# Early loads with one issue per tensor, weight gates from a DMA schedule, and a last tile in two column halves, in a kernel of local attention followed by a two-product MLP

## The chip, the cores and the metric

The kernel runs on one core of one Trainium2 chip. The metric is device time in microseconds (us), as the median of several executions. The "span" of a profile is the time from its first to its last instruction; an execution is about 1.8 us longer than its span.

Engine names in the profile: PE is TensorE's matmuls, PEld its weight loads, DVE is VectorE, ACT is ScalarE, POOL is GpSimd, SP is SyncE. A name with q (SPq, POOLq) is that engine's instruction sequencer, which also issues DMAs.

## The reference

Four batches of 768 positions, eight heads of 64. Each query sees the 96 positions up to itself and the first eight positions of its batch; the result goes through an MLP with `h - tanh(h)` in the middle.

```python
def _attn_ref(q, k, v, n_global, n_local):      # (4, 8, 768, 64), n_global 8, n_local 96
    scores = scale * np.matmul(q, k.transpose(0, 1, 3, 2)) + bias   # bias: -slope(head) * distance
    scores = np.where(keep, scores, -1000000000.0)                  # keep: global or local
    ...                                                             # softmax
    return np.matmul(a, v)

def _moe_ref(x, w_in, w_out):                   # x (3072, 512), w_in (512, 2048), w_out (2048, 512)
    h = x @ w_in
    g = h - np.tanh(h)
    return g @ w_out
```

## The kernel before

The 3072 tokens are 24 tiles of 128. Each tile is loaded as three tensors of 256 KB (keys, queries, values), cast to bf16, transposed on TensorE (early tiles) or by DMA (later tiles), and goes through scores, exponential, product with the values (called AV below), division, transposition, first product with w_in, tanh and difference, and second product with w_out. Each weight matrix comes in four quarters, which GpSimd loads with a cast to bf16 (1 MiB read, 512 KB written, per quarter).

All instructions are ordered by a small planner in the kernel: it simulates the five engines with estimated durations and emits each engine's instructions in the order found. An engine then runs strictly in that order. Three parts matter here. First, the early loads, where keys and queries of the first four tiles are issued as two halves each:

```python
    def load(u, nm, src, dst):
        ...
        if u < PE_B and nm != "vf":          # PE_B = 4
            for a in range(2):
                started(("ld", nm, u), nc.sync.dma_start(
                    out=dst[u][a * Dh : (a + 1) * Dh].rearrange("p t d -> p (t d)"),
                    in_=rows[a * NP : (a + 1) * NP].rearrange("h (k t) d -> k h (t d)", t=H),
                ))
        else:
            started(("ld", nm, u), nc.sync.dma_start(out=dst[u], in_=rows.rearrange("h p d -> p h d")))
```

Second, the order of loads, with "gates": a gated load is issued only when another one has landed. Here the first w_in quarter waits for the fourth tile's keys, and dummy matmuls on a tile of zeros (`warm`) keep TensorE busy before there is work:

```python
    before = [
        ("t", 0), ("t", 1), ("t", 2), ("t", 3), ("in", 0), ("in", 1), ("in", 2), ("in", 3), ("out", 0),
        ("out", 1), ("t", 4), ("out", 2), ("out", 3), ("t", 5), ("t", 6), ("t", 7),
    ]
    ...
    for n, it in enumerate(before):
        if n and it[0] != "t" and before[n - 1][0] == "t":
            gate_of[it] = ("ld", "kf", before[n - 1][1])
        elif n >= 2 and it[0] == "t" and before[n - 1][0] != "t":
            gate_of["ld", "kf", it[1]] = landed(before[n - 2])
```

Third, the end of each tile: sixteen matmuls of 128x512 into one PSUM bank, one copy by ScalarE, one store.

```python
    def m2_e(u):
        ots[u] = opool.tile([P, DM], FP32, name="ot")
        nc.scalar.copy(out=ots[u], in_=os_.pop(u))

    def store(u):
        nc.sync.dma_start(out=out[u * P : (u + 1) * P, :], in_=ots.pop(u))
```

The softmax here doesn't subtract the row's maximum and nothing guards it: scores larger than these inputs give would overflow.

## Time and profile before

| | before |
|---|---|
| median of 3 runs, us | 224.93 (224.05 to 225.29) |
| span of the profiled execution, us | 221.7 |
| first matmul with w_in starts | 21.56 |
| first w_in quarter: issued, landed | 15.8, 21.5 |
| last matmul ends, span ends | 217.86, 221.7 |

From the profile's page, the span and the part "chain that ended last", which is followed back from the last instruction and gives each engine's share:

```profile
span 221.7 us, 5261 instructions
...
PE 85%; DMA 6%; SPq 4%; issue 2%; ACT 1%; POOL 1%; DVE 1%; POOLq 0%
```

TensorE has 85% of the chain. What is not TensorE is at the two ends. The next view is the table of stretches of before; after the stretch and its length come each engine's busy time in us (with its number of instructions), the granted clock of TensorE, the mean busy share of the 16 DMA engines and what they moved:

```profile
core 0: us, PE busy (x) PEld busy (x) DVE busy (x) ACT busy (x) POOL busy (x), PEclk, DMA share, GB/s
...
14.00:16.00 2.00, 1.55 (x17) 0.67 (x16) 1.48 (x4) 1.51 (x2) 1.42 (x3) 1.00 0.78 191
16.00:18.00 2.00, 2.00 (x59) 1.53 (x58) 1.18 (x5) 1.23 (x2) 2.00 (x4) 1.00 0.19 35
18.00:20.00 2.00, 1.95 (x25) 0.98 (x24) 1.28 (x3) 1.41 (x2) 2.00 (x4) 1.00 1.09 172
```

There is a hole: in the stretch from 16 to 18 us the DMA engines are 0.19 busy, although all the weights are still to come. The timeline of GpSimd (start, length, engine, line, operation; in brackets the idle time before it and what ended it) shows why:

```profile
14.39 0.62 POOL L186 CAST vb_107<-vf 128x512 bf16<-128x512 f32 x1 [1.23 <-DMA vf<-in_v_dram]
15.19 0.61 POOL L178 CAST kq<-kf 128x512 bf16<-128x512 f32 x1 [0.19 <-DMA kf<-in_k_dram]
15.75 0.89 POOL L168 DMA_DIRECT2D w_in_bf_97<-in_moe_w_in_dram  x1
```

GpSimd, which must issue the weights, first waits for the third tile's values, casts them, and then waits for the fourth tile's keys. The timeline of TensorE shows the 21 dummies and the late first matmul with w_in:

```profile
1.20 6.22 PE L317 MATMUL one<-zero 128*128 128x512 bf16 x21 [1.20 <-DVE zero L577]
7.34 0.69 PE L198 MATMUL one<-ident,kq 64*64 64x64 bf16 x32
...
21.56 1.08 PE L325 MATMUL one<-xT,w_in_bf_97 128*128 128x128 bf16 x16 [0.82 <-DMA w_in_bf_97<-in_moe_w_in_dram]
```

At the end, the timeline shows the last copy, of 0.58 us, after which the span has another 3.2 us, with the store:

```profile
217.90 0.58 ACT L359 COPY ot<-one 128x512 f32<-128x512 f32 x1 [2.87 <-PE one L352]
```

### The profile page before, as it was taken

What the parts mean: (1) busy time and instruction counts of PE and PEld (TensorE: products, weight loads), DVE (VectorE), ACT (ScalarE), POOL (GpSimd) and SP (SyncE); (2) the same over time, 40 slices, a digit from 0 to 9 for tenths busy, and PEclk for the clock granted to TensorE, in tenths of its full rate; (3) what the DMA queues carried; (4) which work ended last, traced back from release to release, by engine and by line L of the source; (5) the groups of instructions that cost most, each with busy time, mean ns of one, the idle gap of its engine ahead of it and who ended that gap; (6) DMA issues with size and microseconds to landing.
All of it is one profiled execution on the core that took longest, in us unless ns stands there. A gap on an engine that the chain in (4) does not pass through costs nothing.

```text
span 221.7 us, 5261 instructions
## 1 busy us (share of the span) xinstructions
PE 211.8 (96%) x2084; PEld 133.7 (60%) x2113; DVE 135.0 (61%) x278; ACT 127.5 (58%) x212; POOL 52.9 (24%) x85
## 2 busy tenths in 40 slices
PE   7788999999999999999999999999999999999993
PEld 3455897659686566566556555656656555555541
DVE  7246575456788789788886866677566444444300
ACT  5176567837689377575764666656764454534321
POOL 1468003126455453143322323321000000000000
PEclk9999999999999999999999999999999999999999
DMA  4988998999999999999999999993621111001112
GB/s 125 244 202 141 204 216 165 183 213 240 270 230 239 219 231 209 194 206 191 251 173 198 243 214 231 164 234 72 121 71 27 47 47 47 27 27 47 47 65 77
DMA packets 96409, 35.21 MB, mean 159 GB/s; under 512 B 89728, under 2 KB 91776, under 8 KB 96384
## 3 DMA queue, kind: packets, MB, share of 16 engines
q1 hardware_dynamic: 93696, 30.68, 65.5%
q0 software_dynamic: 2688, 4.19, 10.8%
q8 instruction: 16, 0.26, 0.5%
q14 instruction: 9, 0.07, 0.1%
HBM read 27.26 MB, written 6.29 MB: 151 GB/s over the span
## 4 chain that ended last, share of the span: by engine, by line
PE 85%; DMA 6%; SPq 4%; issue 2%; ACT 1%; POOL 1%; DVE 1%; POOLq 0%
PE one L325 38%; PE one L352 37%; PE big L242 5%; DMA w_in_bf_98<-in_moe_w_in_dram 4%; SPq L159 3%; PE big L265 2%; DMA vf<-in_v_dram 2%; PE big L269 2%; PE one L204 1%; PE one L292 1%; SPq L164 1%; POOL kq L178 1%; ACT pd L250 0%; DVE g L342 0%; DVE pd L254 0%
## 5 line engine op out<-in xcount | busy, mean ns | idle before, releaser
L336 ACT ACTIVATE th<-one 128x384 f32<-128x384 f32 (+1 forms) x120 | 61.3, 514 | 52.6 <-PE one L325 51.7
L342 DVE TENSOR_TENSOR g<-one,th 128x384 bf16<-128x384 f32 (+1 forms) x120 | 68.2, 581 | 38.4 <-ACT th L336 37.1
L352 PEld LDWEIGHTS <-g 128*128 128x128 bf16 x384 | 36.2, 98 | 34.3 <-issue 0.2
L180 POOL CAST kq<-kf 128x512 bf16<-128x512 f32 x20 | 13.2, 660 | 72.0 <-DMA kf<-in_k_dram 69.1
L250 ACT ACTIVATE pd<-big 128x1024 bf16<-128x1024 f32 x24 | 24.5, 1025 | 9.9 <-PE big L242 9.8
L325 PE MATMUL one<-xT,w_in_bf_97 128*128 128x128 bf16 (+1 forms) x192 | 25.5, 273 | 0.8 <-DMA w_in_bf_97<-in_moe_w_in_dram 0.8
L325 PE MATMUL one<-xT,w_in_bf_98 128*128 128x128 bf16 (+1 forms) x192 | 25.5, 273 | 0.2 <-DMA w_in_bf_98<-in_moe_w_in_dram 0.2
L325 PE MATMUL one<-xT,w_in_bf_99 128*128 128x128 bf16 (+1 forms) x192 | 25.6, 273 | 0.0
L325 PE MATMUL one<-xT,w_in_bf_100 128*128 128x128 bf16 (+1 forms) x192 | 25.2, 273 | 0.1
L352 PE MATMUL one<-w_out_bf_101,g 128*128 128x512 bf16 x89 | 24.1, 379 | 0.5 <-DVE qk L216 0.2
L359 ACT COPY ot<-one 128x512 f32<-128x512 f32 x24 | 14.1, 588 | 16.9 <-PE one L352 16.7
L352 PE MATMUL one<-w_out_bf_103,g 128*128 128x512 bf16 x90 | 23.5, 379 | 0.3
L352 PE MATMUL one<-w_out_bf_104,g 128*128 128x512 bf16 x89 | 23.3, 379 | 0.5 <-issue 0.2
L352 PE MATMUL one<-w_out_bf_102,g 128*128 128x512 bf16 x90 | 23.4, 379 | 0.3
L254 DVE TENSOR_TENSOR pd<-pd,mk 128x1024 bf16<-128x1024 bf16 x20 | 15.4, 771 | 10.2 <-ACT pd L250 9.9
L250 ACT ACTIVATE po<-big 128x1024 bf16<-128x1024 f32 x20 | 20.5, 1027 | 0.5 <-PE big L242 0.5
L325 PEld LDWEIGHTS <-w_in_bf_97 128*128 128x128 bf16 x192 | 16.1, 114 | 7.0 <-DMA w_in_bf_97<-in_moe_w_in_dram 0.9
L325 PEld LDWEIGHTS <-w_in_bf_100 128*128 128x128 bf16 x192 | 16.3, 113 | 6.4 <-issue 0.2
L325 PEld LDWEIGHTS <-w_in_bf_99 128*128 128x128 bf16 x192 | 16.2, 114 | 6.5
L325 PEld LDWEIGHTS <-w_in_bf_98 128*128 128x128 bf16 x192 | 16.0, 114 | 6.5 <-DMA w_in_bf_98<-in_moe_w_in_dram 0.3
L278 DVE TENSOR_TENSOR x<-big,rden 128x512 bf16<-128x512 f32 x24 | 16.6, 692 | 0.9
L180 POOL CAST kq<-qf 128x512 bf16<-128x512 f32 x20 | 14.2, 711 | 8.2 <-DMA qf<-in_q_dram 8.1
(100 smaller groups left out, 189.3 us busy)
## 6 DMA issues: line engine op xcount, KB each, us to landing
vf<-in_v_dram SPq DMA_DIRECT2D x24, 256.0 KB, 4.5
out_dram<-ot SPq DMA_DIRECT2D x24, 256.0 KB, 2.7
kf<-in_k_dram SPq DMA_DIRECT2D x20, 256.0 KB, 3.6
qf<-in_q_dram SPq DMA_DIRECT2D x20, 256.0 KB, 4.3
kf<-in_k_dram SPq DMA_DIRECT2D x8, 128.0 KB, 3.6
qf<-in_q_dram SPq DMA_DIRECT2D x8, 128.0 KB, 3.4
w_in_bf_97<-in_moe_w_in_dram POOLq DMA_DIRECT2D x1, 512.0 KB, 5.8
w_in_bf_98<-in_moe_w_in_dram POOLq DMA_DIRECT2D x1, 512.0 KB, 8.1
```

Source lines behind the costliest of these rows:

```text
L159: started(("ld", nm, u), nc.sync.dma_start(out=dst[u][a * Dh : (a + 1) * Dh].rearrange("p t d -> p (t d)"), in_=rows[a * NP : (a + 1) * NP ...
L180: eng.tensor_copy(out=kq[u][:, j, :].rearrange("p (c a d) -> p a c d", a=2, d=Dh), in_=t.rearrange("p (a c) d -> p a c d", a=2),)
L242: nc.tensor.matmul(s[:, hh * NP + p, :], qk[u - o][r, 1, p, :], qk[u][r, 0, p, :], start=(u >= PE_B), stop=(u >= PE_B or p == NP - 1),)
L250: nc.scalar.activation(pr[u, o], s, AF.Exp, bias=0.0, scale=scale)
L254: nc.vector.tensor_tensor(out=pr[u, o], in0=pr[u, o], in1=mk[:, :, m, :], op=ALU.mult)
L265: nc.tensor.matmul(dst, pr[u, 0][:, h, :], vb[u % NV][:, h, :], start=True, stop=last,)
L278: nc.vector.tensor_tensor(out=xs[u].rearrange("q (a h) d -> q a h d", a=2), in0=t[:, :, :, 0:Dh], in1=rden.to_broadcast([P, 2, H // 2, Dh] ...
L325: nc.tensor.matmul(t[:, (f - f0) * n : (f - f0 + 1) * n], w_in_bf[j][:, c, i : FJ * P : FJ], xT[b][:, c, o : o + n], start=(c == 0), stop= ...
L336: nc.scalar.activation(h_view(ths[g, f0], g), h_view(hs[g, f0], g), AF.Tanh, bias=0.0, scale=1.0)
L342: nc.vector.tensor_tensor(out=gs[b][:, f0 : f0 + m, o : o + n], in0=h_view(hs.pop((g, f0)), g), in1=h_view(ths.pop((g, f0)), g), op=ALU.su ...
L352: nc.tensor.matmul(os_[u], gs[u // HT][:, f, t * P : (t + 1) * P], w_out_bf[f // FJ][:, f % FJ, :], start=(f == 0), stop=(f == CF - 1),)
L359: nc.scalar.copy(out=ots[u], in_=os_.pop(u))
```

## The change

The intent: give SyncE half as many early issues, so that the DMA engines are kept full; compute the gates from a simple schedule of the DMA engines, so that weights are issued before the last early load has landed; and shorten the end by finishing half of the last tile's columns earlier. With it come settings for the middle (bias by matmul for a fifth tile, transposes by DMA from the tenth tile in place of the eleventh, `AHEAD` 4.5, `EARLY2` 6), and the first w_out quarter moves to second place among the weights. Cut to its core:

```diff
-    PE_B = 4
-    PE_T, PE_X = 10, 10
+    PE_B = 5
+    LB = 4
+    PE_T, PE_X = 9, 9
...
-    EARLY, EARLY2 = 6, 4
+    EARLY, EARLY2 = 6, 6
...
+    BY_ACT = [("qf", 0)]
...
-        if u < PE_B and nm != "vf":
-            for a in range(2):
-                started(("ld", nm, u), nc.sync.dma_start(
-                    out=dst[u][a * Dh : (a + 1) * Dh].rearrange("p t d -> p (t d)"),
-                    in_=rows[a * NP : (a + 1) * NP].rearrange("h (k t) d -> k h (t d)", t=H),
-                ))
+        eng = nc.scalar if (nm, u) in BY_ACT else nc.sync
+        if u < LB and nm != "vf":
+            started(("ld", nm, u), eng.dma_start(
+                out=dst[u].rearrange("p t d -> p (t d)"),
+                in_=rows.rearrange("h (k t) d -> k h (t d)", t=H),
+            ))
...
+    def a_TL(u, j):                     # early transposes, keys and queries apart, as 128x64 matmuls
+        tr[u, j] = ps_one.tile([P, NP * P], FP32, name="one")
+        for t in range(H):
+            for a in range(2):
+                nc.tensor.matmul(
+                    tr[u, j][a * Dh : (a + 1) * Dh, t * Dh : (t + 1) * Dh],
+                    kq[u][:, j, t * Dh : (t + 1) * Dh],
+                    ident.rearrange("p (k a c) -> p a k c", a=2, c=NP)[:, a], start=True, stop=True,
+                )
...
-    AHEAD = 6.0
-    WARM = (1.4, 19.0)
+    AHEAD = 4.5
+    WARM = (1.3, 16.0)
...
-        ("t", 0), ("t", 1), ("t", 2), ("t", 3), ("in", 0), ("in", 1), ("in", 2), ("in", 3), ("out", 0),
+        ("t", 0), ("t", 1), ("t", 2), ("t", 3), ("in", 0), ("out", 0), ("in", 1), ("in", 2), ("in", 3),
...
+    T_LAND, T_SP, T_POOL = 1.0, 1.6, 2.2
+    ends = []
+    at = 2.3
+    for n, it in enumerate(before):
+        first = ("ld", "kf", it[1]) if it[0] == "t" else it
+        if n and (it[0] == "t") != (before[n - 1][0] == "t"):
+            due = at + 0.3 - T_LAND - (T_SP if it[0] == "t" else T_POOL)
+            past = [key for e, key in ends if e <= due]
+            if past:
+                gate_of[first] = past[-1]
+        ...                             # at grows by the estimated transfer; its end goes to `ends`
...
-        e0 = DVE if u == 0 else POOL
-        c0 = 0.5 if u == 0 else 0.62
+        e0, c0 = ((DVE, POOL), (0.48, 0.62)) if u < PE_B else ((POOL,), (0.62,))
...
+        if u == NU - 1:                 # the last tile: two halves of 256 columns
+            for qq in range(4):
+                d, r = divmod(qq, 2)
+                op(("m2", u, qq), PE, 0.88, lambda u=u, d=d, r=r: m2_half(u, d, r), ...)
+            for d, e, us in ((0, ACT, 0.4), (1, DVE, 0.28)):
+                op(("ev", u, d), e, us, lambda u=u, d=d, e=e: m2_half_e(e, u, d), ...)
+                op(("st", u, d), SP, 0.45, lambda u=u, d=d: store_half(u, d), ...)
+            continue
```

With these gates the first w_in quarter waits for the third tile's queries.

More of the change, by code (lines that the diff above doesn't have):

```diff
@@ L154, in load @@
         rows = src[b, :, i * P : (i + 1) * P, :]
-        if u < PE_B and nm != "vf":
-            for a in range(2):
-                started(("ld", nm, u), nc.sync.dma_start(
-                    out=dst[u][a * Dh : (a + 1) * Dh].rearrange("p t d -> p (t d)"),
-                    in_=rows[a * NP : (a + 1) * NP].rearrange("h (k t) d -> k h (t d)", t=H),
-                ))
+        eng = nc.scalar if (nm, u) in BY_ACT else nc.sync
[4 more added lines that the diff above has]
+            ))
         else:
-            started(("ld", nm, u), nc.sync.dma_start(out=dst[u], in_=rows.rearrange("h p d -> p h d")))
+            started(("ld", nm, u), eng.dma_start(out=dst[u], in_=rows.rearrange("h p d -> p h d")))
     def load_w_in(j):
@@ L176, in cast @@
         t = src.pop(u)
-        if u < PE_B:
+        if u < LB:
             eng.tensor_copy(out=kq[u][:, j, :], in_=t.rearrange("p h d -> p (h d)"))
@@ L193, in a_T @@
         for j in (1, 0):
-            if u < PE_B:
-                for t in range(H):
-                    for a in range(2):
-                        r = slice(a * Dh, (a + 1) * Dh)
-                        nc.tensor.transpose(
-                            tr[u][r, j].rearrange("r c f -> r (c f)")[:, t * Dh : (t + 1) * Dh],
-                            kq[u][r, j, t * Dh : (t + 1) * Dh], ident[r, r],
-                        )
-                continue
             for p in range(NP):
                 nc.tensor.transpose(tr[u][:, j, p, :], kq[u][:, j, p * P : (p + 1) * P], ident)
+    def a_TL(u, j):
[7 more added lines that the diff above has]
+                )
     def a_DT(u):
@@ L220, in a_Te @@
             qk[u] = kpool.tile([P, 2, NP, P], BF16, name="qk")
-        if u < PE_B:
+        if u < LB:
             copy(e, out=qk[u][:, j].rearrange("r c (k t) -> r c k t", t=H),
-                 in_=tr[u][:, j].rearrange("r c f -> r (c f)").rearrange(
-                     "r (t k c) -> r c k t", t=H, c=NP))
+                 in_=tr.pop((u, j)).rearrange("r (t k c) -> r c k t", t=H, c=NP))
         else:
@@ L355, in m2, with m2_half, m2_half_e, store_half @@
             )
+    def m2_half(u, d, r):
+        if r == 0:
+            os_[u, d] = ps_one.tile([P, DM], FP32, name="one")
+        t = u % HT
+        w = DM // 2
+        for f in range(r * CF // 2, (r + 1) * CF // 2):
+            nc.tensor.matmul(
+                os_[u, d][:, 0:w], gs[u // HT][:, f, t * P : (t + 1) * P],
+                w_out_bf[f // FJ][:, f % FJ, d * w : (d + 1) * w], start=(f == 0), stop=(f == CF - 1),
+            )
+    def m2_half_e(e, u, d):
+        w = DM // 2
+        ots[u, d] = opool.tile([P, w], FP32, name=f"oh{d}")
+        copy(e, out=ots[u, d], in_=os_.pop((u, d))[:, 0:w])
+    def store_half(u, d):
+        w = DM // 2
+        nc.sync.dma_start(out=out[u * P : (u + 1) * P, d * w : (d + 1) * w], in_=ots.pop((u, d)))
     def m2_e(u):
@@ L369 @@
     before = [
-        ("t", 0), ("t", 1), ("t", 2), ("t", 3), ("in", 0), ("in", 1), ("in", 2), ("in", 3), ("out", 0),
+        ("t", 0), ("t", 1), ("t", 2), ("t", 3), ("in", 0), ("out", 0), ("in", 1), ("in", 2), ("in", 3),
         ("out", 1), ("t", 4), ("out", 2), ("out", 3), ("t", 5), ("t", 6), ("t", 7),
     ]
-    def landed(it):
-        return ("ld", "vf", it[1]) if it[0] == "t" else it
     tiles = [it[1] for it in before if it[0] == "t"]
+    T_LAND, T_SP, T_POOL = 1.0, 1.6, 2.2
[8 more added lines that the diff above has]
+                gate_of[first] = past[-1]
+        if it[0] == "t":
+            for nm in ("kf", "qf", "vf"):
+                at += T_LD if it[1] >= LB or nm == "vf" else T_LD8
+                ends.append((at, ("ld", nm, it[1])))
+        else:
+            at += T_W[it[0]]
+            ends.append((at, it))
     for u in range(NU):
@@ L381 @@
             tiles.append(u)
-    for n, it in enumerate(before):
-        if n and it[0] != "t" and before[n - 1][0] == "t":
-            gate_of[it] = ("ld", "kf", before[n - 1][1])
-        elif n >= 2 and it[0] == "t" and before[n - 1][0] != "t":
-            gate_of["ld", "kf", it[1]] = landed(before[n - 2])
     prev = None
@@ L409 @@
             key = ("ld", nm, u)
-            op(key, SP, 0.55 if u >= PE_B or nm == "vf" else 0.8, lambda u=u, nm=nm, src=src, dst=dst: load(u, nm, src, dst),
-               after=[gate_of.get(key), prev and ("issue", prev)], take=[nm], dma=T_LD if u >= PE_B or nm == "vf" else T_LD8)
+            by_act = (nm, u) in BY_ACT
+            op(key, SP, 0.0 if by_act else 0.62,
+               (lambda: None) if by_act else lambda u=u, nm=nm, src=src, dst=dst: load(u, nm, src, dst),
+               after=[gate_of.get(key), prev and ("issue", prev)], take=[nm], dma=T_LD if u >= LB or nm == "vf" else T_LD8)
             prev = key
@@ L414 @@
         i = u % NQ
-        e0 = DVE if u == 0 else POOL
-        c0 = 0.5 if u == 0 else 0.62
-        op(("ck", u), e0, c0, lambda u=u, e=e0: cast(u, 1, kf, nc.vector if e is DVE else nc.gpsimd),
+        e0, c0 = ((DVE, POOL), (0.48, 0.62)) if u < PE_B else ((POOL,), (0.62,))
+        op(("ck", u), e0, c0, lambda e, u=u: cast(u, 1, kf, nc.vector if e is DVE else nc.gpsimd),
            after=[("ld", "kf", u)], take=["kq"], give=["kf"], pri=-1)
-        op(("cq", u), e0, c0, lambda u=u, e=e0: cast(u, 0, qf, nc.vector if e is DVE else nc.gpsimd),
+        op(("cq", u), e0, c0, lambda e, u=u: cast(u, 0, qf, nc.vector if e is DVE else nc.gpsimd),
            after=[("ld", "qf", u), ("ck", u)], give=["qf"], pri=-1)
@@ L424 @@
         go = [key for a, key in prog if a <= u - AHEAD]
-        tdep = [("ck", u), ("cq", u), ("issue", ("T", u - 1)) if u else None, go[-1] if go else None]
-        if u < PE_T:
-            op(("T", u), PE, 0.7 if u < PE_B else 0.46, lambda u=u: a_T(u), after=tdep, take=["one"], give=["kq"])
+        before_T = [("issue", ("T", u - 1)) if u else None, go[-1] if go else None]
+        tdep = [("ck", u), ("cq", u)] + before_T
+        if u < LB:
+            for j, c in ((1, "ck"), (0, "cq")):
+                op(("T", u, j), PE, 0.44, lambda u=u, j=j: a_TL(u, j), after=[(c, u)] + before_T, take=["one"])
+                op(("Te", u, j), (DVE, ACT), (0.7, 0.6), lambda e, u=u, j=j: a_Te(u, j, e), after=[("T", u, j)],
+                   give=["one"])
+            op(("Te", u, 2), DVE, 0.0, lambda: None, after=[("Te", u, 0), ("Te", u, 1)])
+            op(("T", u), PE, 0.0, lambda: None, after=[("T", u, 0), ("T", u, 1)], give=["kq"])
+        elif u < PE_T:
+            op(("T", u), PE, 0.46, lambda u=u: a_T(u), after=tdep, take=["one"], give=["kq"])
             for j in (1, 0):
@@ L434 @@
         for o in (0, 1) if i else (0,):
-            op(("S", u, o), PE, 0.69 if u < PE_B else 0.24, lambda u=u, o=o: a_S(u, o),
+            op(("S", u, o), PE, 0.72 if u < PE_B else 0.24, lambda u=u, o=o: a_S(u, o),
                after=[te, "bias" if u < PE_B else None, ("K", u - 1) if o and i >= 2 else None], take=["big"])
@@ L472 @@
         m = shape1(g)[3]
+        if u == NU - 1:
+            for qq in range(4):
+                d, r = divmod(qq, 2)
+                op(("m2", u, qq), PE, 0.88, lambda u=u, d=d, r=r: m2_half(u, d, r),
+                   after=[("out", WJ - 1), ("g", g, (8 * r + 7) // m * m)], take=["one"] if r == 0 else [], pri=2)
+            for d, e, us in ((0, ACT, 0.4), (1, DVE, 0.28)):
+                op(("ev", u, d), e, us, lambda u=u, d=d, e=e: m2_half_e(e, u, d), after=[("m2", u, 2 * d + 1)],
+                   give=["one"], pri=1)
+                op(("st", u, d), SP, 0.45, lambda u=u, d=d: store_half(u, d), after=[("ev", u, d)], dma=T_ST / 2)
+            continue
         for qq in range(4):
@@ L485, in plan @@
         avail = {n: [0.0] * c for n, c in bufs.items()}
-        free = {PE: WARM[0], ACT: 5.3, DVE: 5.1, POOL: 1.9, SP: 0.7}
+        free = {PE: WARM[0], ACT: 5.2, DVE: 4.6, POOL: 1.9, SP: 0.7}
         avail["one"][0] = WARM[1]
@@ L541, in plan @@
                 dma_free = max(dma_free, end + (1.0 if o["eng"] is SP else 1.3)) + o["dma"]
-                done[key] = dma_free + 0.6
+                done[key] = dma_free + 1.0
             else:
@@ L566, in with_warm @@
         for t in pe:
-            us = 0.43 if t < 6.0 else 0.22
-            while last + us + 0.08 <= min(t, WARM[1]):
+            while True:
+                us = 0.43 if last < 4.8 else 0.22
+                if last + us + 0.08 > min(t, WARM[1]):
+                    break
                 ops["warm", n] = dict(eng=PE, us=us, fn=warm)
@@ L576 @@
     with tc.manual_schedule(engines={PE, ACT, DVE, POOL, SP}):
+        for nm, u in BY_ACT:
+            load(u, nm, {"kf": k, "qf": q, "vf": v}[nm], {"kf": kf, "qf": qf, "vf": vf}[nm])
         nc.vector.memset(zero, 0.0)
+        for i in range(NV):
+            nc.vector.memset(vb[i][:, :, Dh : Dh + 1], 1.0)
+        build_masks()
         make_identity(nc, ident)
-        build_masks()
         for h in range(H):
             bias(h)
-        for i in range(NV):
-            nc.vector.memset(vb[i][:, :, Dh : Dh + 1], 1.0)
         for t, key in with_warm(order):
```

## The prediction

> **What bounds it now.** The table of busy time by stretches shows TensorE full (98.4 to 99.5%) from 27.5 us on, at full granted clock; in the chain of waits 85% is TensorE. So time is lost only at the ends.
>
> Start: by the timeline the first real first-product matmul begins at 21.56 us, when the first quarter of w_in lands. Before it TensorE does some 11 us of attention for four tiles; the rest is dummies and waiting. Three things make it late. (a) SyncE's queue spends 1.2 us on each early key or query pair (two half issues of 0.59), 3.1 us a tile; by stretches of 1 us the DMA engines are 0.92 busy from 2 to 16 us, against 1.2 when weights stream. (b) the first w_in issue waits for the fourth tile's keys (15.75); the DMA share falls to 0.2 between 16 and 18. (c) 21 dummies hold TensorE to 7.34, though the casts were done at 6.1.
> End: last matmul ends at 217.86; eviction 0.58, then a 256 KB store; 3.8 us in all.
>
> **What the change does.**
> 1. One issue per early key/query tensor, the first query by ScalarE: about 1.85 us a tile, so the loads become DMA-bound. The Trainium skill (Trainium Kernel Development and Optimization, Key Constraints) says several engines' queues share the same 16 DMA engines and only issue time is saved; the shares above agree. Estimate from 280 GB/s at the busiest microseconds: 0.93 us a tensor, eight tensors by about 10 us, four tiles by 13 instead of 16 to 17.6.
> 2. The first weight's gate is now the third tile's queries (about 10 us). First bytes come 2.3 us after the issue began, then 3.5 to 4 us: it lands near 16.4 instead of 21.56.
> 3. Attention is the second limit: VectorE shares the casts, fewer dummies, but TensorE's order keeps the same attention (through the third tile's product with V) ahead of the first w_in matmul. With exponentials of 1.03 us in a chain on ScalarE I get 17.3 us. From there weights (3.1 us per w_in, 2.5 per w_out quarter, w_out's first now second) arrive about as fast as TensorE uses them; small new waits are likely.
> 4. Costs: bias by matmul for tile 4 adds 0.86 us; tile 9 transposed by DMA takes off 0.7. The 64x64 transposes become as many 128x64 matmuls: even.
> 5. Last tile in halves: same matmul time; last eviction 0.3 instead of 0.58 and a 128 KB store: 0.55 us off.
>
> **On the critical path.** Start 21.56 to about 17.3: 4.3 us; end 0.55; cost 0.2. Together 4.6: **220.3 us**, 8 in 10 between 218.6 and 222.2. Faster by over 2%: 0.52; within 2%: 0.47; slower by over 2%: 0.01. It stands on the 2% line (220.4).
>
> **What would show it.** Right: early issues 0.6 us each; DMA share 1.1 or more from 3 us on, no hole at 16 to 18; first w_in issue near 10, landing near 16.4; first first-product matmul at 16.5 to 18; the fifth tile's transposes (now at 40.5) near 35; stretches after 60 us as full as before; last matmul to end of span about 3.2.
> Wrong: first w_in matmul kept by ScalarE or VectorE past 18.5; loads still landing every 1.05 us; small value packets slowed by weight packets, so that the fourth tile's attention is late; TensorE waits on w_in's second quarter, w_out's second or third quarter or the fifth tile's keys, giving the gain back between 20 and 45 us.
>
> **What would make it wrong.** The gain equals the start's shift only if later stretches stay full. Weight landings that slip 1 us cost that directly. If attention keeps up with the weight's landing (16.4), 219.4.

## The result, and the profile after

| | before | after |
|---|---|---|
| median, us (5 runs each, same chip) | 225.16 (224.05 to 225.39) | 222.34 (221.43 to 222.60) |
| ratio of the means | | 0.9875, 95% interval 0.9842 to 0.9908 |
| span of the profiled execution, us | 221.7 | 220.7 |
| first matmul with w_in starts | 21.56 | 20.80 |
| first w_in quarter: issued, landed | 15.8, 21.5 | 12.8, 20.5 |
| last matmul ends to span ends | 3.8 | 3.2 |

Every ratio in this document is the mean time of one kernel's fast runs over the mean of the other's fast runs of the same rounds, so it is not quite the ratio of the medians quoted. The change is faster by 1.25%, and the class is "same" at the 2% threshold. The measured 222.34 lies 0.14 us above the predicted range of 218.6 to 222.2, and 2 us above the predicted 220.3.

The page of after, span and chain:

```profile
span 220.7 us, 5274 instructions
...
PE 82%; DMA 11%; DVE 3%; ACT 1%; POOL 1%; issue 0%; SPq 0%; POOLq 0%; DVEq 0%
```

SyncE's issuing (SPq) has left the chain, as intended. The DMA engines have more of it, but not in its place: of their 24.5 us on the chain 4.75 lie at the start, and the rest between 46.7 and 58.8 and between 97.7 and 106.2 us, in loads of later tiles and a transpose. The stretches of after:

```profile
14.00:16.00 2.00, 2.00 (x33) 0.95 (x29) 1.28 (x4) 2.00 (x3) 2.00 (x4) 1.00 1.24 220
16.00:18.00 2.00, 2.00 (x59) 1.53 (x58) 1.89 (x4) 1.63 (x3) 2.00 (x4) 1.00 1.25 208
18.00:20.00 2.00, 1.78 (x19) 0.69 (x19) 1.48 (x4) 1.45 (x2) 0.16 (x1) 1.00 1.18 224
```

The hole is gone: 1.25 in place of 0.19. GpSimd issues the first weight three microseconds earlier, having waited for the third tile's queries:

```profile
12.76 0.90 POOL L169 DMA_DIRECT2D w_in_bf_97<-in_moe_w_in_dram  x1 [1.81 <-DMA qf<-in_q_dram]
```

Yet the first matmul with w_in moved by 0.76 us only. The page's list of DMA issues (size, and us from issue to landing) for that first quarter, of before and of after:

```profile
w_in_bf_97<-in_moe_w_in_dram POOLq DMA_DIRECT2D x1, 512.0 KB, 5.8
```

```profile
w_in_bf_97<-in_moe_w_in_dram POOLq DMA_DIRECT2D x1, 512.0 KB, 7.8
```

It was issued 3.0 us earlier and took 2.0 us longer. And in the timeline of TensorE of after, no wait stands before that matmul, although its operand had landed only at 20.5:

```profile
1.20 3.17 PE L319 MATMUL one<-zero 128*128 128x512 bf16 x7 [1.20 <-DVE zero L634]
6.21 1.06 PE L203 MATMUL one<-ident,kq 128*64 128x64 bf16 x32 [1.85 <-POOL kq L179]
7.21 2.31 PE L319 MATMUL one<-zero 128*128 128x512 bf16 x5
9.32 1.06 PE L237 MATMUL big<-bm,ident 128*128 128x512 bf16 x2
...
20.76 0.20 PE L271 MATMUL big<-vb_106,po 128*128 128x65 bf16 x1
20.80 1.06 PE L327 MATMUL one<-xT,w_in_bf_97 128*128 128x128 bf16 x16
```

TensorE came to it straight from the third tile's AV. So the weight and the attention chain arrived together: two limits within 0.3 us. In the chain of waits of after, cut to its first 11 us, one sees what the attention chain consists of (start, length, what):

```profile
0.74 4.75 DMA kf<-in_k_dram
...
6.21 1.06 PE one L203 x18
7.28 2.25 PE one L319 x5
9.52 0.85 PE big L237 x2
```

The five dummies, 2.25 us, are on the chain, and one starts 0.42 us after the other (five from 7.21 to 9.32), where before's 21 took 0.30 on average. TensorE ran at half clock: seven dummies did not last until there was work, and it idled for 1.85 us. The Trainium skill, "TensorE: Matmul & The Clock Gate", Part 1, says that the array starts at half its clock and is released after a window of about 3.4 us of activity, with 426.7 ns a 512-column matmul cold and 215.7 ns warm. This agrees on the durations: 0.42 us against the 0.215 us that a second-product matmul of that width takes later (four in 0.86 us). The granted clock of the table of stretches says 1.00 throughout all this, so it doesn't show a clock that was not yet released; the durations do.

The end of after:

```profile
217.59 0.42 DVE L219 COPY oh_3524<-one 128x256 f32<-128x256 f32 x1 [8.46 <-PE one L366]
218.04 0.33 SPq L378 DMA_DIRECT2D out_dram<-oh_3524  x1
```

### A measure that all runs share

The pair of profiles differs by 1.0 us, the medians by 2.8. The profile of before happened to fall on a fast execution: that one took 223.46 us, and all 44 executions of before that ran beside the experiments lie between 223.83 and 227.23 (the six of e1, the same kernel, between 223.59 and 226.40). So one pair of profiles is not enough to place the gain. TensorE's busy time is no good measure either: the page of before has 2084 matmuls to 2113 weight loads, so 29 matmul records are missing there, and what looks idle may be a missing record.

I therefore use a working-out of my own: the TensorE time lost, which is the time passed minus the time that the matmuls started so far need at the full rate seen in the full stretches, taken from the starts of the weight loads. It is good to some tenths, and only its differences are used. The whole work is 201.5 us before and 201.7 us after (the cost that the prediction named), so span = work + lost. By part of the span:

| kernel | what it is | lost by 30 us | 30 to 215 us | 215 us to end | ratio to before |
|---|---|---|---|---|---|
| before | profile above | 12.4 | 3.5 | 4.3 | |
| e1 | before, again | 12.7 | 4.9 | 4.4 | 0.9976 |
| after | profile above | 11.6 | 3.8 | 3.6 | 0.9875 |
| e5 | after, again | 10.8 | 3.9 | 3.5 | 0.9869 |
| e3 | new loads only | 12.1 | 4.8 | 4.4 | 0.9956 |
| e4 | after, whole tail | 11.5 | 4.2 | 4.0 | 0.9864 |
| e11 | after, old gates | 11.9 | 5.2 | 3.6 | 0.9964 |
| e10 | before, new gates | 12.3 | 7.5 | 4.3 | 1.0127 |
| e8 | before, new middle | 12.1 | 5.9 | 4.3 | 1.0062 |
| e6 | after, more dummies | 11.1 | 3.7 | 3.5 | 0.9859 |
| e7 | after, fewer bytes | 11.0 | 3.7 | 3.5 | 0.9825 |
| e9 | e6 and e7 together | 9.2 | 4.1 | 2.8 | 0.9754 |
| e12 | first weight before the fourth tile | 11.4 | 6.7 | 3.7 | 1.0008 |
| e13 | e12, second weight before it too | 11.7 | 7.8 | 3.8 | 1.0091 |
| e14 | e6, values behind keys and queries | 13.4 | 5.9 | 3.7 | 1.0086 |

Against e1, the more usual execution of before, the change takes 1.1 to 1.9 us off the first 30 us, about 1 us off the middle and 0.8 off the end, and adds 0.2 us of work. (In e9 the last matmul ends at 214.6, before the cut at 215, so some 0.4 us of its end stand in the middle column.)

### The profile page after: what moved, and what is told of

Its sections match the earlier page's. It is cut to its first block, busy times and chain, and to the rows that moved or that the text cites. A ratio compares the mean times of both kernels' runs of the same rounds, so it can differ in the third digit from the quotient of the medians.

```text
span 220.7 us, 5274 instructions
## 1 busy us (share of the span) xinstructions
PE 213.5 (97%) x2108; PEld 134.2 (61%) x2108; DVE 132.1 (60%) x277; ACT 128.6 (58%) x215; POOL 48.5 (22%) x79
## 4 chain that ended last, share of the span: by engine, by line
PE 82%; DMA 11%; DVE 3%; ACT 1%; POOL 1%; issue 0%; SPq 0%; POOLq 0%; DVEq 0%
PE one L327 33%; PE one L354 32%; DMA kf<-in_k_dram 5%; PE big L244 5%; DMA qf<-in_q_dram 3%; DMA qk<-kq 3%; PE big L267 2%; PE big L271 2%; PE big L237 2%; PE one L366 2%; PE one L203 1%; PE one L319 1%; PE one L294 1%; ACT th L338 1%; DVE x L280 1%; DVE qk L219 1%
## 5 line engine op out<-in xcount | busy, mean ns | idle before, releaser
L354 PEld LDWEIGHTS <-g 128*128 128x128 bf16 x368 | 34.6, 98 | 32.4
L327 PE MATMUL one<-xT,w_in_bf_100 128*128 128x128 bf16 (+1 forms) x192 | 25.7, 273 | 0.0
L327 PE MATMUL one<-xT,w_in_bf_99 128*128 128x128 bf16 (+1 forms) x192 | 25.2, 273 | 0.0
L327 PE MATMUL one<-xT,w_in_bf_98 128*128 128x128 bf16 (+1 forms) x192 | 24.8, 273 | 0.3 <-DVE g L344 0.3
L327 PE MATMUL one<-xT,w_in_bf_97 128*128 128x128 bf16 (+1 forms) x192 | 24.6, 273 | 0.0
L181 POOL CAST kq<-kf 128x512 bf16<-128x512 f32 x19 | 13.4, 707 | 50.6 <-DMA kf<-in_k_dram 39.5
L382 ACT COPY ot<-one 128x512 f32<-128x512 f32 x23 | 13.5, 587 | 18.6 <-PE one L354 18.6
L252 ACT ACTIVATE po<-big 128x1024 bf16<-128x1024 f32 x20 | 20.5, 1024 | 0.8 <-PE big L244 0.7
L256 DVE TENSOR_TENSOR pd<-pd,mk 128x1024 bf16<-128x1024 bf16 x19 | 13.3, 698 | 12.2 <-ACT pd L252 12.0
L327 PEld LDWEIGHTS <-w_in_bf_97 128*128 128x128 bf16 x192 | 16.2, 114 | 5.8
L244 PEld LDWEIGHTS <-qk 64*128 64x128 bf16 x352 | 10.0, 95 | 11.1 <-issue 9.1
```

Source lines behind the costliest of these rows:

```text
L181: eng.tensor_copy(out=kq[u][:, j, :].rearrange("p (c a d) -> p a c d", a=2, d=Dh), in_=t.rearrange("p (a c) d -> p a c d", a=2),)
L244: nc.tensor.matmul(s[:, hh * NP + p, :], qk[u - o][r, 1, p, :], qk[u][r, 0, p, :], start=(u >= PE_B), stop=(u >= PE_B or p == NP - 1),)
L252: nc.scalar.activation(pr[u, o], s, AF.Exp, bias=0.0, scale=scale)
L256: nc.vector.tensor_tensor(out=pr[u, o], in0=pr[u, o], in1=mk[:, :, m, :], op=ALU.mult)
L327: nc.tensor.matmul(t[:, (f - f0) * n : (f - f0 + 1) * n], w_in_bf[j][:, c, i : FJ * P : FJ], xT[b][:, c, o : o + n], start=(c == 0), stop= ...
L354: nc.tensor.matmul(os_[u], gs[u // HT][:, f, t * P : (t + 1) * P], w_out_bf[f // FJ][:, f % FJ, :], start=(f == 0), stop=(f == CF - 1),)
```

## The experiments

The theories, named here by what they say. Theory "bytes": the early loads were bound by the DMA engines already, so fewer issues don't bring them in sooner, and the first weight, issued earlier, only shares the engines. Theory "chain": the attention chain on TensorE, ScalarE and VectorE, begun late at half clock, holds the first matmul with w_in. Theory "two limits" (D in the expectations): both at the same time, so that removing one alone gains nothing. Theory "gates": the gain that there is comes from filling the hole in the DMA engines. Rival to it, theory "middle" (C in the expectations): it comes from the settings of the middle and not from the start at all. The expectations call "bytes" A, "chain" B (in e2 and e3, B is the single issues and the attention behind them) and "gates" E.

Kernels e1 to e14 ran, each beside its own runs of before.

### e1: before, again

No edit. It shows how far two profiles of one kernel differ.

> Null control: the kernel before, unchanged. Every theory expects a ratio of 1.000 within 0.5%. It also gives a second profile: the first one of before (span 221.7) lies 1 to 2 us under the spans that its timed runs imply, so I expect a span of about 223 here, and want to see in which stretch the difference lies (guess: TensorE waits between 40 and 80 us, where loads share the DMA engines).

Measured: 225.36 us, ratio 0.9976 (0.9934 to 1.0019). The span is 223.5, 1.8 us more than the first profile's, and two causes can be seen. TensorE fell to half clock from 14.6 to 18.1 us (its timeline has the two 512-column bias matmuls at 14.52 in 0.93 us, and such a pair in 0.60 at full clock), and in the table of waits of TensorE (who waited for what, us in total, times, longest) from 60 to 82 us stands the first tile that is transposed by DMA:

```profile
engine line waited for: us in total, times, longest us
PE big L242 <- DMA qk<-kq: 1.3, 1, 1.3
```

The first profile of before has no wait over 0.2 us there. So part of before's usual time is a wait that comes and goes.

### e2: before, first weight gated on the third tile's queries

```diff
+    gate_of["in", 0] = ("ld", "qf", 2)
```

> The kernel before with one thing changed: the first w_in load waits for the third tile's queries instead of the fourth tile's keys. Theory A (the early loads were bound by the DMA engines already, so only the gate moves data forward): first w_in issue near 12.6 us, landing near 20, first first-product matmul near 20.5 instead of 21.56, and 0.7 to 1.5 us off the total, most of the whole change's start gain. Theory B (the gain comes from the loads in one issue and the attention that follows them): under 0.4 us.

Measured: 226.81 us over six executions, one of them slow (226.69 over the five fast ones), ratio of the fast ones 1.0045 (1.000 to 1.009). It isn't faster, though the gate is the changed kernel's, so the 0.7 to 1.5 us that theory A expected did not come.

### e3: the new loads alone

The changed kernel with the gates, weight order, middle settings and tail of before. Short diff against the changed kernel:

```diff
-    PE_B = 5
+    PE_B = 4
-    PE_T, PE_X = 9, 9
+    PE_T, PE_X = 10, 10
-    EARLY, EARLY2 = 6, 6
+    EARLY, EARLY2 = 6, 4
-    AHEAD = 4.5
+    AHEAD = 6.0
...                                  # order of the weights and gates as in before
-        if u == NU - 1:
+        if False:
```

> The changed kernel with only the new early loads (one issue a tensor, first queries by ScalarE, casts shared with VectorE, transposes by tensor, fewer dummies); gates, order of weights, fifth tile and last tile as in the kernel before. Theory A: the third tile's queries still land at 12.5 to 12.7 us and the fourth tile's keys near 15, so first w_in issue is no earlier than about 15 and the total is within 0.5 us of before. Theory B, and my prediction: tiles land 2 to 3 us sooner, and 1.5 to 3 us come off.

Measured: 224.56 us, ratio 0.9956 (0.9923 to 0.9988): the single issues, the separate transposes and the shared casts give 0.4%, and the first matmul with w_in starts at 22.54, no earlier than before. The loads alone don't move the start. Theory A had the landings right (third tile's queries at 12.2, first weight issued at 15.2); in time, 1.0 us came off, between what A and B allowed. In this profile TensorE was at half clock from 11.8 to 15.2 us, so the start of 22.54 is that of one execution.

### e4: after, with the whole last tile

```diff
-        if u == NU - 1:
+        if False:
```

> The changed kernel with the last tile's second product in one piece again. From the two profiles (end of last matmul to end of span 3.1 against 3.8 us) all theories expect it 0.5 to 0.8 us slower than the changed kernel, ratio to before about 0.991. If it is as fast as the changed kernel, the halves are worth nothing.

Measured: 222.81 us, ratio 0.9864 (0.9829 to 0.9899). The halves can be seen in every profile: from 215 us to the end, 4.0 us are lost here and 3.5 to 3.6 with halves. In the total times they can't be resolved: 0.9864 here, and 0.9869 and 0.9875 for the changed kernel, whose intervals are 0.7% wide.

### e5: after, again

No edit.

> Control: the changed kernel unchanged, on the chip of this call. Ratio to before 0.987 plus or minus 0.004; first first-product matmul again at 20.5 to 21 us, with the third tile's queries landed near 12.5 and the first w_in quarter near 20.5. Beside the kernel with the whole last tile (0.986 in the last call) it tells whether the halves show in the time at all.

Measured: 221.75 us, ratio 0.9869 (0.9828 to 0.9910), span 219.9. TensorE reached full clock at 9.8 us, not at 12.2 as in the first profile of after; the first matmul with w_in came at 19.96. It is the same kernel, so the start moves by 0.8 us between executions, and the traces show two differences: the clock, and loads that landed 0.3 to 0.8 us earlier (the twelfth tensor at 16.4 and not 17.2).

### e6: after, with eight more early dummies

```diff
+            if t >= 4.0 and ("extra", 0) not in ops:
+                for i in range(8):
+                    ops["extra", i] = dict(eng=PE, us=0.22, fn=warm)
+                    order.append((t - 0.001, ("extra", i)))
```

> The changed kernel with 8 more dummies before the first transposes, so that TensorE does not idle from 4.4 to 6.2 us and should be at full clock from about 5 us on instead of from 12. Theory B (the attention chain, slowed by TensorE's half clock, sets the start): products with V of the third tile end 1 us or more sooner and 1 to 2 us come off the total. Theory A (DMA engines set it): the first w_in quarter still lands near 20.5, the first first-product matmul stays within 0.4 us of 20.8 and the total within 0.5 us of the changed kernel.

Measured: 221.80 us, ratio 0.9859 (0.9826 to 0.9891). From the timeline of TensorE:

```profile
1.19 5.66 PE L319 MATMUL one<-zero 128*128 128x512 bf16 x15 [1.19 <-DVE zero L638]
...
8.50 0.59 PE L237 MATMUL big<-bm,ident 128*128 128x512 bf16 x2
...
20.22 0.97 PE L327 MATMUL one<-xT,w_in_bf 128*128 128x128 bf16 x14
```

The warm-up does what it should: the first scores' bias starts at 8.50 in place of 9.32 and takes 0.59 in place of 1.06. But the first matmul with w_in is at 20.22. Theory "chain" alone falls. The weight landed at 20.2 too, but the chain of waits of e6 shows what had taken back the gain:

```profile
8.65 7.08 DMA qf<-in_q_dram
...
15.75 0.17 DVE kq L179
...
17.70 0.70 DVE x L280
```

The chain runs over SyncE's issues to the fourth tile's queries, which landed at 15.7, and over their cast on VectorE, which stands there ahead of the second tile's division; the transposes of that division's result stand on TensorE ahead of the third tile's AV. In the chain of the changed kernel no load but that of the first keys stands ahead of the first matmul with w_in. So the limit behind the half clock is the landing of the early loads, and not that of the weight.

### e7: after, with fewer bytes (wrong result)

The values of the first four tiles are loaded for one head only and copied to the others, which takes 7/8 of four tensors of 256 KB off the DMA engines.

```diff
+            n = 1 if u < LB and nm == "vf" else H
-            started(("ld", nm, u), eng.dma_start(out=dst[u], in_=rows.rearrange("h p d -> p h d")))
+            started(("ld", nm, u), eng.dma_start(out=dst[u][:, 0:n], in_=rows[0:n].rearrange("h p d -> p h d")))
...                                  # the cast of the values copies that head to all eight
```

> WRONG RESULT on purpose: of the value tensors of the first four tiles only one head in eight is loaded (and copied to the others), same instructions in the same order; 0.9 MB fewer bytes in small packets before the first weight. Theory A: third tile's queries land near 10 to 10.5 instead of 12.5, first w_in quarter near 17 instead of 20.5, first first-product matmul near 17.5 to 18.5, and 2 to 3.5 us come off the total, close to what I had predicted for the change. Theory B: the loads come sooner, but the first first-product matmul does not start before about 20, and under 1 us comes off.

Measured: 221.54 us, ratio 0.9825 (0.9788 to 0.9862); relative error 0.51, as meant. The first weight lands at 17.6, almost 3 us earlier than in the changed kernel. The first matmul with w_in still starts at 20.20. Theory "bytes" alone falls too. (The ratio is 0.4% under the changed kernel's, with overlapping intervals; the time lost in the three parts of the span is e5's to 0.2 us.)

### e8: before, with the middle settings of after

```diff
-    PE_B = 4
-    PE_T, PE_X = 10, 10
+    PE_B = 5
+    LB = 4
+    PE_T, PE_X = 9, 9
-    EARLY, EARLY2 = 6, 4
+    EARLY, EARLY2 = 6, 6
-    AHEAD = 6.0
+    AHEAD = 4.5
...                                  # elsewhere PE_B becomes LB, so that the loads stay as in before
```

> The kernel before with only the settings for the middle of the kernel: bias by matmul also for the fifth tile, the tenth tile transposed by DMA instead of TensorE, six tiles' second products in the early order, transposes let ahead 4.5 instead of 6 tiles. Theory C (a good part of the measured gain came from here, because TensorE no longer waits 0 to 2 us at about 77 us for the first DMA-transposed tile): 0.5 to 1.5 us faster than before, no such wait between 60 and 80 us. If the middle settings are only a cost of 0.2 us, as I had predicted, it is within 0.3 us of before or slower.

Measured: 226.39 us, ratio 1.0062 (1.0028 to 1.0097): these settings alone cost 0.6%, 1.4 us. The wait for the first DMA-transposed tile is still there, 1.5 us in the waits of TensorE from 60 to 82 us. Theory "middle" falls as a cause by itself; whether these settings help beside the new gates was not run.

### e9: more dummies and fewer bytes together (wrong result)

The edits of e6 and e7.

> WRONG RESULT on purpose: the changed kernel with both of the last call's edits, 8 more dummies and seven eighths of the first four tiles' value bytes left out. Each alone left the first first-product matmul at 20.2 us. Theory D (two limits that end at the same time: landings, and the hand-over chain of attention that starts late because TensorE is at half clock): with both taken away it starts at 18 to 18.7 us, and the total is 1.3 to 2 us below the changed kernel (ratio to before about 0.979). If it stays at 20, the chain from the first exponential on is the limit whatever starts it.

Measured: 219.55 us, ratio 0.9754 (0.9715 to 0.9794). The first matmul with w_in:

```profile
18.34 1.06 PE L329 MATMUL one<-xT,w_in_bf 128*128 128x128 bf16 x16
```

Each alone left it at 20.2; both together bring it to 18.34. In TensorE time lost by 30 us, the dummies alone leave 11.1, the bytes alone 11.0, both 9.2. This is what "two limits" says, and neither of the single theories. The starts are of one execution each and that of the changed kernel moved by 0.8 us between two, but the total stands clear as well: 0.9754 against e6's 0.9859, intervals apart, some 2.4 us, a little more than was expected. In none of after, e5, e6, e7 and e9 does a wait for the weight stand before the first matmul with w_in.

### e10: before, with the new gates and weight order

The block that computes the gates, and the order of the weights, moved into before; nothing else.

```diff
-        ("t", 0), ("t", 1), ("t", 2), ("t", 3), ("in", 0), ("in", 1), ("in", 2), ("in", 3), ("out", 0),
+        ("t", 0), ("t", 1), ("t", 2), ("t", 3), ("in", 0), ("out", 0), ("in", 1), ("in", 2), ("in", 3),
...                                  # the gates from the DMA schedule, as in the change
```

> The kernel before with the whole new order of the DMA queue and nothing else: gates from the schedule and the first w_out quarter second. Theory E (the gain comes from keeping the DMA engines full between 16 and 40 us, so that everything later lands 2 us sooner, also the first DMA-transposed tile at 77 us): last w_out quarter lands near 43 instead of 45 to 46, and 1 to 2.5 us come off. If it is within 0.5 us of before, the gates need the new loads or the middle settings to pay.

Measured: 228.21 us, ratio 1.0127 (1.0078 to 1.0176), the slowest of all. The weight is issued at 13.0 and the first matmul with w_in starts at 19.91, earlier than in the changed kernel. But in this kernel GpSimd alone casts the fourth tile's keys and queries, and it does so between the weight issues: the second w_in quarter is issued only at 16.0, and the fourth tile's values, in competition with the weights, land at 23.7 (16.7 in before). TensorE waits for the casts in its waits up to 60 us:

```profile
PE one L198 <- POOL kq L178: 1.9, 2, 1.2
```

The expected 1 to 2.5 us did not come. An earlier start alone is worth nothing if it is paid for later: 7.5 us are lost from 30 to 215 us, the highest but one in the table.

### e11: after, with the old gates and weight order

```diff
-        ("t", 0), ("t", 1), ("t", 2), ("t", 3), ("in", 0), ("out", 0), ("in", 1), ("in", 2), ("in", 3),
+        ("t", 0), ("t", 1), ("t", 2), ("t", 3), ("in", 0), ("in", 1), ("in", 2), ("in", 3), ("out", 0),
...                                  # gates as in before
```

> The changed kernel with the old gates and the old order of the weights. Theory E: last w_out quarter again at 44 to 46 us, the wait for the first DMA-transposed tile back (0.5 to 2 us between 60 and 80 us), and the total 1.5 to 2.5 us slower than the changed kernel (ratio to before 0.994 to 1.0). If the gates are not what matters, it stays at 0.987.

Measured: 224.51 us, ratio 0.9964 (0.9930 to 0.9998), against 0.9875 and 0.9869 with the new gates: they are worth about 0.9%, 2 us, inside the changed kernel. Of that, about 0.3 to 1.1 us is in the first 30 us of the table and 1.4 us from 30 to 215. Most of the latter falls between 60 and 80 us, where e11 loses 2.8 us and the changed kernel 0.5; e11's waits of TensorE from 60 to 82 us, of which the changed kernel's list is empty:

```profile
PE one L294 <- ACT xT L217: 0.8, 1, 0.8
PE one L294 <- DVE g L344: 0.3, 1, 0.3
```

So the gates and the order of the weights, tested together and not apart, are worth this much inside the changed kernel. The path that theory "gates" named, that everything later lands 2 us sooner, is not shown: e11's last w_out quarter landed at 43.2, and the changed kernel's at 43.0. e10 adds a condition, argued from its waits: only with loads and casts that leave GpSimd free to issue. As the new loads and gates were not run with the old middle settings, these may belong to the condition too.

### e12: a start made for both limits, correct result

An attempt to have e9's start in a correct kernel: e6's dummies; the order of the early loads k0, q0, k1, q1, v0, k2, q2, v1, v2 (keys, queries, values of tile n); the first w_in quarter gated on the third tile's keys and put ahead of the fourth tile's loads.

```diff
-        ("t", 0), ("t", 1), ("t", 2), ("t", 3), ("in", 0), ("out", 0), ("in", 1), ...
+        ("t", 0), ("t", 1), ("t", 2), ("in", 0), ("t", 3), ("in", 1), ("out", 0), ...
...
+    gate_of["in", 0] = ("ld", "kf", 2)
+    gate_of["ld", "kf", 3] = ("ld", "vf", 2)
+    gate_of["in", 1] = ("ld", "kf", 3)
```

> An attempt to beat both: the changed kernel with 8 more dummies, the first three tiles' queries and keys ahead of their values, and the first w_in quarter loaded ahead of the fourth tile. By theory D the first w_in quarter lands near 17 and the first first-product matmul starts at 17 to 18 us instead of 20.2; if the later weights come as before, 1.5 to 2.5 us off the changed kernel (ratio to before about 0.978). If the total does not move, the time is given back in waits for w_in's second quarter or the fourth tile before 35 us.

Measured: 225.18 us, ratio 1.0008 (0.9962 to 1.0054). The first matmul with w_in starts at 17.54, as intended and as the prediction had wanted of the change. All of it was given back: 6.7 us are lost from 30 to 215 us, 2.9 us more than in the changed kernel, and by 30 us the gain had already gone (11.4 lost against 11.6). Its waits up to 60 us are for VectorE (1.0 us for differences, 1.0 for a division), and none is for the second weight.

### e13: the same, with the second weight moved as well

With e13 and e14 I asked why the start of e12 came to nothing. This one asks whether e12 lost it for its late second weight (issued at 18.1, landed at 23.4).

```diff
-        ("t", 0), ("t", 1), ("t", 2), ("in", 0), ("t", 3), ("in", 1), ("out", 0), ...
+        ("t", 0), ("t", 1), ("t", 2), ("in", 0), ("in", 1), ("t", 3), ("out", 0), ...
...
-    gate_of["in", 1] = ("ld", "kf", 3)
+    gate_of["in", 1] = ("ld", "qf", 2)
```

> The start kernel again (early dummies, values behind keys and queries, first w_in quarter ahead of the fourth tile's loads), but the second w_in quarter now goes with the first and the fourth tile's loads wait behind both. If what that kernel gave back came from its weights arriving late (its second w_in quarter had been gated on the fourth tile's keys), the first w_in matmul stays near 17.5 us, the second quarter lands by 21.5 and the time falls to about 0.976 of before, 220 us. If instead it came from VectorE and ScalarE, which have to serve the fourth tile's attention and the two groups of first products at the same time, the waits for x and g at 22 to 35 us stay and it stays at 0.99 to 1.00.

Measured: 226.80 us, ratio 1.0091 (1.0055 to 1.0126). The timeline of TensorE:

```profile
16.77 1.98 PE L327 MATMUL one<-xT,w_in_bf 128*128 128x128 bf16 x32
...
21.24 1.09 PE L327 MATMUL one<-xT,w_in_bf 128*128 128x128 bf16 x16 [2.01 <-DMA w_in_bf<-in_moe_w_in_dram]
```

The earliest start of all, 16.77, and 2.0 us of waiting right after it, because the second quarter landed at 21.2. It came when expected (21.5) and even so too late for a start at 16.8. The fourth tile's values, behind it, landed at 25.4 (17.2 in the changed kernel), and two waits for VectorE and ScalarE, of 0.5 and 0.7 us, stand at 32.5 and 33.5. So an earlier second weight doesn't give the start back, which speaks against the first of the two explanations; the time is worse than the second one allowed for as well.

### e14: values behind keys and queries, weights as in the change

```diff
+    loads = [(0, "kf"), (0, "qf"), (1, "kf"), (1, "qf"), (0, "vf"), (2, "kf"), (2, "qf"), (1, "vf"), (2, "vf")]
+    loads += [(u, nm) for u in tiles if u > 2 for nm in tensors]
...
+    gate_of["in", 0] = ("ld", "kf", 2)
+    gate_of["out", 0] = ("ld", "vf", 2)
```

(on top of e6's dummies)

> The changed kernel with the eight early dummies, values of the first three tiles behind keys and queries, and the first w_in quarter gated on the third tile's keys; the fourth tile is still loaded unhindered and the weight order is the changed kernel's. A correct kernel that moves both limits a little. If start is set by both the attention chain and the first weight, the first w_in matmul comes 0.5 to 1.5 us before that of the changed kernel with dummies (20.2), at 18.7 to 19.7, and the time is 0.979 to 0.985 of before. If the DMA engines alone set it, the weight shares them with the fourth tile, lands at 20 or later as before, and the ratio stays at 0.986 to 0.988.

Measured: 226.53 us, ratio 1.0086 (1.0047 to 1.0125), a miss of both expectations. The first matmul with w_in started at 22.40. The first weight landed at 19.0, 1.2 us earlier than in e6, but it slowed the fourth tile: its queries landed at 17.2 (15.7 in e6) and its values at 25.6 (17.7). TensorE, whose order has the fourth tile's transposes ahead of the first matmul with w_in, waited for their cast:

```profile
16.67 0.44 PE L203 MATMUL one<-ident,kq 128*64 128x64 bf16 x16 [2.32 <-DVE kq L179]
```

Around this wait it fell to half clock, from 17.4 to 20.9 us, so part of this execution's late start is the clock's.

### What the landings say together

All these kernels load the same four tiles (12 tensors) and weight quarters in the same 26 us, in different orders. When were all 12 tensors and three of the weight quarters on the chip?

| kernel | first w_in quarter landed | 12 tensors and 3 quarters landed |
|---|---|---|
| before | 21.5 | 27.9 |
| after | 20.5 | 25.5 |
| e6 | 20.2 | 25.2 |
| e12 | 17.1 | 25.9 |
| e13 | 16.7 | 25.4 |
| e14 | 19.0 | 25.6 |
| e9 (0.9 MB less) | 16.2 | 22.1 |

In the kernels with all bytes, after to e14, the order moves the first weight by 4 us and the sum by 0.7. The DMA engines deliver 6.3 MB by about 25.5 us whatever stands first, and what one kernel gets early it pays for with the next thing it needs. Before is 2.4 us later in this column than after. With the new loads and the old gates, which leave part of the hole, it is 26.8 (e3) and 26.4 (e11), and the changed kernel again (e5) has 24.8, so some 1 to 2 us of it are the new gates'. The column alone doesn't set the time: e10, the slowest kernel, has 25.5. An estimate from these numbers: 6.3 MB from about 2 us, where the trace of before has the first DMA traffic, to 25.5 are some 270 GB/s.

The Trainium skill, "DMA: Bandwidth & Descriptors", section "Issuing engines are not separate DMA queues", says that DMAs started by several engines run on the same 16 DMA engines and interleave, and that starting them from more engines saves issue time only, "which is usually small relative to the DMA itself". This agrees that the issue time saved brought nothing in sooner, though an early issue, 0.6 us, isn't small beside the pace of landing: the twelve tensors of the four tiles landed in 12.6 us before (from 4.1 to 16.7) and in 12.8 us after (from 4.4 to 17.2), one every 1.15 us in both. Before, SyncE's 3.1 us of issues a tile were nearly as slow as that pace, and the last query landed 3.4 us after its issue; after, 7.1 us, so there the tensors wait at the DMA engines.

No correct kernel of these beats the change. e6, with 0.9859, can't be told from it.

## Why the prediction was right or wrong

- **"so the loads become DMA-bound ... 0.93 us a tensor, eight tensors by about 10 us, four tiles by 13 instead of 16 to 17.6".** This is the step that failed first. SyncE's issue did fall to 0.6 us a tensor, and the loads were bound by the DMA engines, but at 1.1 us for a key or query tensor and 1.3 for a value tensor. The eighth tensor landed at 12.5, the twelfth at 17.2, and before had the same twelve at 16.7. The rate of 280 GB/s was read off the busiest microseconds; sustained over the loads it is lower (256 KB in 1.15 us are 228 GB/s). The share of 0.92 that the prediction quotes from 2 to 16 us is 0.85 in the stretches of before. e3 shows the value of this step by itself: 0.4%.
- **"lands near 16.4 instead of 21.56".** It landed at 20.5. The gate opened 2.5 us late, for the reason above, and the weight then took 7.8 us from issue to landing where the prediction had some 6, since it shared the engines with the fourth tile (5.6 us in e9, where most of the value bytes are gone). The prediction cited the skill for exactly this sharing ("Trainium Kernel Development and Optimization", Key Constraints) and applied it to the issue time but not to the weight's own flight.
- **"Attention is the second limit ... I get 17.3 us".** That it is the second limit was right. Its size wasn't: it came at 20.8 in the profiled run and about 20 in e5. Two causes are shown: TensorE at half clock with five dummies of 0.42 us in the chain, and keys, queries and values that landed at the DMA engines' pace (by e6's chain, the fourth tile's queries, at 15.7 where the prediction had all four tiles by 13). Removing the first (e6) or cutting the bytes (e7) leaves the start at 20.2; removing both (e9) gives 18.3. Even then it isn't 17.3.
- **"the end 0.55, cost 0.2".** Both are right by the profiles: 3.8 to 3.2 us from the last matmul to the end, 201.5 to 201.7 us of work. The end can't be resolved in total times. The cost is right as work only: on the kernel before, the middle settings cost 1.4 us (e8).
- **"stretches after 60 us as full as before".** They are fuller than in a usual run of before: between 60 and 80 us e1 loses 2.9 us, the changed kernel 0.5. This the prediction did not count. It read a profile of before that was faster than any of 44 later executions and that lacks the 1.3 us wait for the first DMA-transposed tile. e11 puts the gates' worth at about 2 us of the 2.8.
- **The sum.** Predicted: 4.3 us at the start. Measured: 0.8 in the first matmul with w_in between the two profiles, 1.1 to 1.9 in time lost by 30 us. What kept the total near was a gain in the middle that was not predicted. The list of what would be wrong had named it: "loads still landing every 1.05 us" is what happened.

What stays open. Why the loss at 60 to 80 us depends on gates that act before 35 us is shown as an effect (e11) and not as a mechanism: the waits there are of different kinds in e1, e8 (a DMA transpose) and e11 (ScalarE and VectorE), and e11's 1.1 us of waits are less than half of the 2.8 us lost. The change also altered the planner's own estimates (a load is taken to be on the chip 1.0 us after its transfer, and not 0.6), which can reorder any engine; no run separates that. And whether some other order of TensorE's work could use an early first weight without waiting for the second is not shown; e12 to e14 kept the planner's rules.

## What to carry to other kernels

Before counting an earlier issue as an earlier landing, count the bytes that must land first, at the rate seen over the whole loading phase and not in its best microsecond. If two limits lie within half a microsecond of each other, an experiment that removes only one can show nothing, so remove both together before dropping either. And profile the kernel before twice: here one lucky profile hid a wait that made up a good part of the later gain.

## What the Trainium skill lacked or had wrong

- "TensorE: Matmul & The Clock Gate", Part 1: right as far as these runs show (0.42 us from one cold 512-column matmul to the next, 0.215 warm, and a moment of release that varies: 12.2 and 9.8 us in two executions of the changed kernel). It says that the ramp costs under 1% of a typical span, which holds here too (e6 and e5, without and with the ramp in the real work, differ by 0.1%). It gives no number for an idle gap inside the warm-up. Here, of six profiles whose first dummies were followed by 1.8 to 1.9 us of idling, five show the release at 9.8 to 12.2 us (e3's is at 5.0); the ten without this gap show it at 3.9 to 7.2. The table's granted clock reads 1.00 before the release.
- The same page's section "A second HAM failure mode: psum-queue depth-cycling" does tell of a clock that falls back through short idles, but not of how much idling is enough. Here e1 ran at half clock from 14.6 to 18.0 us (granted clock 0.50 from 15 to 18), after waits of 1.2 and 0.5 us and with TensorE busy for 0.56 us of the 2 us from 12 to 14; e3 and e14 show such a fall too.
- "DMA: Bandwidth & Descriptors", section "Issuing engines are not separate DMA queues": agrees, but the section gives no number for a transfer that shares the engines. Here the first weight quarter (512 KB written) took 5.8 us from issue to landing behind loads that were nearly done, and 7.8 us beside a tile's loads.
- "Perfetto Trace Analysis", section "Identifying the Most-Contended Engine", warns that the DMA engines' busy share misleads. This agrees, with a number that the page lacks: from 2 to 14 us the share rose from 0.86 to 1.13, while the engines moved 228 and 226 GB/s and the tensors landed no faster.
